# Retention and two MLPs on one core: the powers of lambda by running sums, the decay table through ScalarE's DMA queue, and a small factor table for r

## The chip, the cores and the metric

One core of a Trainium2 chip runs the whole program. The metric is device microseconds of that core; lower is better. A value is the median of several executions.

## The reference

Inputs q, k, v are [2 batches, 8 heads, 768 positions, 64], `lam` holds one decay per head (0.97 to 0.99), and two MLPs follow.

```python
Dmask = np.where(rel >= 0, lam[:, None, None] ** rel[None, :, :], 0.0)
...
intra = np.einsum('bhic,bhjc->bhij', qb, kb) * Dmask[None]
intra = np.einsum('bhij,bhjd->bhid', intra, vb)
inter = np.einsum('bhid,bhde->bhie', qb * lam_pow[None], kv_state)
out[:, :, sl] = intra + inter
kb_dec = kb * rev_pow[None]
kv_state = lam_block[None, :, None, None] * kv_state + np.einsum('bhsd,bhse->bhde', kb_dec, vb)
...
h = x @ w_in                                   # first MLP, 512 -> 2048
g = np.maximum(h, 0.0) + alpha * np.minimum(h, 0.0)
return (g @ w_out)                             # 2048 -> 512; the second MLP squares relu(h)
```

## The kernel before

Retention is done first, in 12 chunks n = 0 to 11 (six chunks of 128 positions for two batches, in turn). The two MLPs follow on the 1536 rows that retention left in SBUF as a high and a low part.

The names of one chunk: `k`, `q` (channels first) and `v`, `r` (positions first; `r` is k once more) are loads of 256 KB each on SyncE's queue. PE makes scores `s` (L422). DVE multiplies them by the decay table `dec` into `sc` (L434). PE multiplies `sc` by `v` into `o` (L459), adds the state's part from `q` times `grow` (L467), and makes the state's update `pk` from `r` and `v` (L477). ScalarE casts `o` to `xah` (L486), PE subtracts that from `o` (`less`, L495) and ScalarE casts the rest to `xal`. GpSimd multiplies `q` by `grow` (L441) and `r` by the last column of `dec` (L444).

The tables come from `lam`, which is loaded first. VectorE makes lambda^1, ^2, ^4 .. ^128 by seven squarings, corrects their rounding (L357 to L371), and multiplies them out into `z`, 8 rows (heads) of 256: 127 zeros and lambda^0 .. ^128. `z` goes to DRAM as `zd`, and `dec` is read back from there: partition p takes each head's 128 values from place p on, so 1024 pieces of 512 bytes. `grow` is made by PE from `z` (`pg`, L402) and copied out of PSUM by VectorE (L406).

The order on each engine is that of the code; nothing is rescheduled. SyncE and ScalarE issue the DMAs written for them in their own order, and an instruction that waits holds up all that stands behind it on its engine. A DMA raises one of eight semaphores, DMAHW0 to DMAHW7, given in turn; the next DMA on the same semaphore waits until the one before it on that semaphore has landed. The scores have two PSUM buffers, so `s` of chunk 2 waits until ScalarE has copied `s` of chunk 0 (L427). The load of `v` of chunk 1 waits for a one-column GpSimd copy of `grow` (L305), and so for `grow`; all loads of later chunks stand behind it on SyncE. `keep_warm(1)` puts 17 matmuls on zeros ahead of the first `o`.

Of the kernel before, what the change touches and what calls it, by code (L numbers as in the profile page):

```python
# [7 lines left out]
F32 = mybir.dt.float32  # L8
F32R = mybir.dt.float32r
# [3 lines left out]
ALU = mybir.AluOpType  # L13
PSUM = bass.MemoryType.PSUM

B, H, S, D = 2, 8, 768, 64
CH = 128
NCH = S // CH
NN = B * NCH
NPAIR = H // 2  # L20
# [6 lines left out]
ZW = 256  # L27
# [13 lines left out]
ORDER = [(n // B, n % B) for n in range(NN)]  # L41

LEAST = 2.0**-15
WARM = 12, 17
EARLY_UNITS = [0, 0, 0, 1, 0, 1, 0, 1, 0, 1, 1, 0]
EARLY_LOADS = [0, 1, 1, 0, 1, 0, 1, 0, 1, 1, 1, 1]

# [6 lines left out]
def retention_then_two_mlps(  # L54
# [15 lines left out]
    nc = tc.nc  # L70
# [199 lines left out]
    ap1 = actx.enter_context(tc.tile_pool(name="ap1", bufs=1))  # L270
# [6 lines left out]
    pso = actx.enter_context(tc.tile_pool(name="pso", bufs=2, space=PSUM))  # L277
# [3 lines left out]

    lam_sb = ap1.tile([H, 1], F32, name="lam_sb")
    nc.sync.dma_start(lam_sb, lam)
    NB = 8
    sq = ap1.tile([H, NB], F32, name="sq")
    z = ap1.tile([H, ZW], F32, name="z")
    nc.vector.memset(z[:, 0 : CH - 1], 0.0)
    ones, tens = ap1.tile([H, 8], F32, name="ones"), ap1.tile([H, 16], F32, name="tens")
    err = ap1.tile([H, NB], F32, name="err")
    nc.vector.memset(err[:, 0:1], 0.0)  # L290
    nc.vector.memset(ones[:, 0:1], 1.0)
    nc.vector.memset(tens[:, 0:1], 1.0)
    qk_t, vk_t = {}, {}

    def load_qk(n):
# [6 lines left out]
    def load_vk(n):  # L302
        v_t = kp.tile([128, H, D], F32, tag="v", name=f"v{n}")
        if n == 1:
            nc.gpsimd.tensor_copy(v_t[:, 0, 0:1], grow[:, 0, 0:1])  # L305
        nc.sync.dma_start(v_t, vr[n])
        r_t = None
        if ORDER[n][0] < NCH - 1:
            r_t = kp.tile([128, H, D], F32, tag="r", name=f"r{n}")
            nc.sync.dma_start(r_t, kr[n])  # L310
        vk_t[n] = v_t, r_t


    warm = ap1.tile([128, CH], F32, name="warm")
    nc.gpsimd.memset(warm, 0.0)

    def keep_warm(i):
        pw = pso.tile([128, NPAIR, CH], F32, tag="o", name=f"warm_ps{i}")
        for a in range(WARM[i]):
            nc.tensor.matmul(pw[:, a % NPAIR, :], warm, warm, start=True, stop=True)  # L320

    def where(name, shape, pattern, base, fill, channel=1):

        x = ap1.tile(shape, F32, name=name)
        zeros = warm[0 : shape[0], 0 : shape[-1]]
        if len(shape) == 3:
            zeros = zeros.unsqueeze(1).to_broadcast(shape)
        nc.gpsimd.affine_select(
            x, zeros, pattern=pattern, compare_op=ALU.not_equal, fill=fill, base=base,
            channel_multiplier=channel,  # L330
        )
        return x
# [6 lines left out]
    for t in range(2):  # L339
        m = where(f"head{t}", [H, NPAIR, D], [[-2, NPAIR], [0, D]], -t, 1.0)  # L340
        nc.gpsimd.tensor_copy(head[:, :, t], m)

    keep_warm(0)
    for n in range(FIRST):
        load_qk(n)

    nc.vector.tensor_copy(sq[:, 0:1], lam_sb)
    for b in range(1, NB):
        nc.vector.tensor_tensor(sq[:, b : b + 1], sq[:, b - 1 : b], sq[:, b - 1 : b], ALU.mult)
    top = ap1.tile([H, NB - 1], F32R, name="top")  # L350
    topf = top.bitcast(F32)
    low = ap1.tile([H, NB - 1], F32, name="low")
    twice = ap1.tile([H, NB], F32, name="twice")
    tmp = ap1.tile([H, NB - 1], F32, name="tmp")
    tmp2 = ap1.tile([H, NB - 1], F32, name="tmp2")
    a, p = sq[:, 0 : NB - 1], sq[:, 1:NB]
    nc.vector.tensor_copy(top, a)  # L357
    nc.vector.tensor_scalar(twice, sq, 2.0, None, ALU.mult)
    nc.vector.tensor_tensor(tmp, topf, topf, ALU.mult)
    nc.vector.tensor_tensor(low, a, topf, ALU.subtract)  # L360
    nc.vector.tensor_tensor(tmp, tmp, p, ALU.subtract)
    nc.vector.scalar_tensor_tensor(tmp2, low, 2.0, topf, ALU.mult, ALU.mult)
    nc.vector.tensor_tensor(tmp, tmp, tmp2, ALU.add)
    nc.vector.tensor_tensor(tmp2, low, low, ALU.mult)
    nc.vector.tensor_tensor(err[:, 1:NB], tmp, tmp2, ALU.add)
    for b in range(2, NB):
        nc.vector.scalar_tensor_tensor(
            err[:, b : b + 1], err[:, b - 1 : b], twice[:, b - 1 : b], err[:, b : b + 1],
            ALU.mult, ALU.add,
        )  # L370
    nc.vector.tensor_tensor(sq, sq, err, ALU.add)  # L371

    for b in range(4):
        for part, b0 in ((tens, 3), (ones, 0)):
            w = 1 << b
            if w < part.shape[1]:
                nc.vector.tensor_scalar(
                    part[:, w : 2 * w], part[:, 0:w], sq[:, b0 + b : b0 + b + 1], None, ALU.mult
                )
    nc.vector.tensor_tensor(  # L380
        z[:, CH - 1 : 2 * CH - 1].rearrange("h (i j) -> h i j", j=8),
        tens.unsqueeze(2).to_broadcast([H, 16, 8]),
        ones.unsqueeze(1).to_broadcast([H, 16, 8]),
        ALU.mult,
    )
    nc.vector.tensor_copy(z[:, ZW - 1 : ZW], sq[:, NB - 1 : NB])


    zd = dram.tile([H, ZW], F32, name="zd")
    dec = ap1.tile([128, H, CH], F32, name="dec")  # L390
    nc.sync.dma_start(zd, z)
    load_vk(0)
    nc.sync.dma_start(dec, bass.AP(zd[:, :].tensor, zd[:, :].offset, [[1, 128], [ZW, H], [1, CH]]))
    dec_v = dec.rearrange("p (a t) i -> p t a i", t=2)

    grow = ap1.tile([128, NPAIR, CH], F32, name="grow")

    def growth():
        pg = psk.tile([128, 2, NPAIR, D], F32, tag="pk", name="pg")
        pg = pg.rearrange("p a b c -> p (a b c)").rearrange("p (a i) -> p a i", i=CH)  # L400
        for a in range(NPAIR):
            nc.tensor.matmul(  # L402
                pg[:, a], head[:, a].rearrange("h t d -> h (t d)"), z[:, CH:ZW], start=True,
                stop=True,
            )
        nc.vector.tensor_copy(grow, pg)  # L406


    state = {}
# [26 lines left out]
    def factors(n):  # L436

        c = ORDER[n][0]
        if c > 0:
            q_t = qk_t[n][0]  # L440
            nc.gpsimd.tensor_tensor(q_t, q_t, grow, ALU.mult)  # L441
        if c < NCH - 1:
            r_t = vk_t[n][1]
            nc.gpsimd.tensor_tensor(  # L444
                r_t, r_t, dec[:, :, CH - 1 : CH].to_broadcast([128, H, D]), ALU.mult
            )

    old_t = {}
# [63 lines left out]
    for n in range(FIRST):  # L512
        scores(n)
        if n == 2:
            growth()
    keep_warm(1)
    load_vk(1)
    for n in range(2):
        factors(n)
    for n in range(DA):  # L520
        decay(n)
    for n in range(NN):
# [25 lines left out]
        if n + 2 < NN:  # L548
            factors(n + 2)
# [19 lines left out]
    for s in range(len(steps) + LAG):  # L569
        if s < len(steps):  # L570
            m, t, f, part = steps[s]
# [78 lines left out]
```

## Time and profile before

| | |
|---|---|
| median of 3 runs | 588.88 us (587.77 to 589.57) |
| span of the profiled execution | 585.6 us |
| PE busy | 578.3 us (99% of the span) |
| VectorE, ScalarE, GpSimd busy | 360.8, 296.3, 28.2 us |
| retention, up to the first matmul of the MLPs | 58.1 us |

The span runs from the first to the last instruction. The profiled execution's own time is not listed apart from its span; the median of the runs is 3.3 us above the span, which is what lies around it. Busy time is modelled for PE (its matmuls are pipelined), so the argument reads starts of matmuls rather than busy shares.

### The profile page before, as it was taken

The page shows a single profiled execution, that of the slowest core. Times are in us where ns is not written, and L with a number is a line of the kernel's source. Part 1 is how long each engine was busy: PE and PEld are TensorE (multiplying, and loading weights), DVE is VectorE, ACT ScalarE, POOL GpSimd, SP SyncE. Part 2 cuts the span into 40 slices and gives each one's busy share as a digit, 9 for nine tenths or more (in the row PEclk, how much of TensorE's full clock was granted, in tenths as well). Part 3 has the DMA queues.
Part 4 walks back from the last instruction along what each step waited for, and adds up shares of the span by engine and source line. Part 5 has one row for each costly group of instructions (what it writes and reads, how often), then busy time and mean ns, then how long its engine had stood idle before and what let it go on. Part 6 is the DMA issues. An engine that isn't in the chain of part 4 may idle for free.

```text
span 585.6 us, 7998 instructions
## 1 busy us (share of the span) xinstructions
PE 578.3 (99%) x3083; PEld 478.8 (82%) x3083; DVE 360.8 (62%) x616; ACT 296.3 (51%) x515; POOL 28.2 (5%) x31
## 2 busy tenths in 40 slices
PE   8999999999999999999999999999999999999997
PEld 8788788888888888888888888888888888888885
DVE  4787897677677777887887787676622222222422
ACT  2556768676646666576576564654522221322220
POOL 1862000000000000000000000000000000000000
PEclk9999999999999999999999999999999999999999
DMA  7992234322626232332432133332100000400401
GB/s 247 383 390 99 85 131 144 144 78 102 213 78 213 108 98 83 131 119 75 137 115 96 49 108 104 112 109 72 73 0 1 0 1 0 144 0 1 143 1 72
DMA packets 25733, 62.39 MB, mean 107 GB/s; under 512 B 2904, under 2 KB 3936, under 8 KB 25696
## 3 DMA queue, kind: packets, MB, share of 16 engines
q1 hardware_dynamic: 17632, 32.53, 15.7%
q10 hardware_dynamic: 8064, 29.36, 14.5%
q8 instruction: 24, 0.39, 0.3%
q14 instruction: 13, 0.11, 0.1%
HBM read 52.44 MB, written 9.45 MB: 106 GB/s over the span
## 4 chain that ended last, share of the span: by engine, by line
PE 92%; DVE 3%; DMA 2%; ACT 2%; issue 0%; ACTq 0%; DVEq 0%
PE h L172 43%; PE acc L225 22%; PE acc L227 22%; PE o L459 1%; PE o L467 1%; DMA dec<-zd 1%; DMA v<-in_vr_dram 1%; PE s L422 1%; PE pk L477 1%; DVE sc L434 1%; DVE bits L139 0%; PE o L495 0%; ACT bits L122 0%; ACT raw L123 0%; DVE bits L131 0%
## 5 line engine op out<-in xcount | busy, mean ns | idle before, releaser
L191 ACT CAST gh<-g 128x512 fp32r<-128x512 f32 x96 | 59.6, 621 | 92.6 <-DVE g L182 38.6
L182 DVE SCALAR_TENSOR_TENSOR g<-h,g 128x512 f32<-128x512 f32 x48 | 33.2, 691 | 117.2 <-ACT g L181 117.2
L181 ACT ACTIVATE g<-h 128x512 f32<-128x512 f32 x48 | 28.7, 597 | 124.9 <-PE h L172 124.9
L196 DVE TENSOR_TENSOR gl<-g,gh 128x512 fp32r<-128x512 f32 x96 | 66.5, 693 | 31.0 <-ACT gh L191 22.3
L225 PE MATMUL acc<-gh,wl 128*128 128x512 f32 x192 | 74.8, 390 | 0.7 <-ACT gh L191 0.7
L225 PE MATMUL acc<-gl,wh 128*128 128x512 f32 x192 | 74.8, 390 | 0.0
L172 PE MATMUL h<-xah,wl 128*128 128x512 f32 x192 | 74.8, 390 | 0.0
L225 PE MATMUL acc<-gh,wh 128*128 128x512 f32 x192 | 74.7, 389 | 0.0
L172 PE MATMUL h<-xah,wh 128*128 128x512 f32 x192 | 74.7, 389 | 0.0
L172 PE MATMUL h<-xal,wh 128*128 128x512 f32 x192 | 74.7, 389 | 0.0
L172 PE MATMUL h<-xbh,wl 128*128 128x512 f32 x192 | 74.7, 389 | 0.0
L172 PE MATMUL h<-xbl,wh 128*128 128x512 f32 x192 | 74.7, 389 | 0.0
L172 PE MATMUL h<-xbh,wh 128*128 128x512 f32 x192 | 74.7, 389 | 0.0
L227 PE MATMUL acc<-wl,gh 128*128 128x512 f32 x192 | 74.7, 389 | 0.0
L227 PE MATMUL acc<-wh,gh 128*128 128x512 f32 x192 | 74.7, 389 | 0.0
L227 PE MATMUL acc<-wh,gl 128*128 128x512 f32 x192 | 74.7, 389 | 0.0
L186 DVE SCALAR_TENSOR_TENSOR g<-h,g 128x512 f32<-128x512 f32 x42 | 29.0, 691 | 40.7 <-ACT g L185 40.5
L150 DVE TENSOR_TENSOR wl<-bits,wh 128x512 fp32r<-128x512 f32 x64 | 45.2, 706 | 3.9 <-ACT wh L141 3.8
L131 DVE SCALAR_TENSOR_TENSOR bits<-raw,bits 128x512 uint32<-128x512 uint32 x64 | 45.1, 705 | 2.2
L139 DVE CUSTOM_DVE_ANT_0 bits<-raw,bits 128x1024 uint16<-128x1024 uint16 x64 | 45.2, 707 | 0.0
L122 ACT ACTIVATE bits<-raw 128x512 f32<-128x512 f32 x64 | 43.1, 674 | 0.0
L225 PEld LDWEIGHTS acc<-gh,wl 128*128 128x128 f32 x192 | 36.0, 187 | 8.5 <-ACT gh L191 1.1
(81 smaller groups left out, 828.7 us busy)
## 6 DMA issues: line engine op xcount, KB each, us to landing
raw<-in_w_dram ACTq DMA_DIRECT2D x56, 512.0 KB, 3.3
ps<-sums SPq DMA_DIRECT2D x24, 256.0 KB, 3.3
sums<-p SPq DMA_DIRECT2D x20, 256.0 KB, 2.2
raw<-in_w_dram SPq DMA_DIRECT2D x8, 512.0 KB, 6.0
k<-in_kt_dram SPq DMA_DIRECT2D x12, 256.0 KB, 4.9
q<-in_qt_dram SPq DMA_DIRECT2D x12, 256.0 KB, 5.3
v<-in_vr_dram SPq DMA_DIRECT2D x12, 256.0 KB, 5.9
r<-in_kr_dram SPq DMA_DIRECT2D x10, 256.0 KB, 5.3
```

Source lines behind the costliest of these rows:

```text
L122: nc.scalar.activation(x.bitcast(F32), high.bitcast(F32), AF.Abs)
L131: nc.vector.scalar_tensor_tensor(x, high, 0xC0000000, x, ALU.bitwise_and, ALU.bitwise_or)
L139: nc.vector.tensor_tensor(x.bitcast(I32), x.bitcast(I32), low.bitcast(I32), ALU.add)
L150: nc.vector.tensor_tensor(lo, x, hi.bitcast(F32), ALU.subtract)
L172: nc.tensor.matmul(ph, w[:, cols], x[:, c, :], start=c == 0 and i == 0, stop=c == NC - 1 and i == 2)
L181: nc.scalar.activation(g, ph, AF.Relu)
L182: nc.vector.scalar_tensor_tensor(g, ph, 0.0, g, ALU.max, ALU.mult)
L186: nc.vector.scalar_tensor_tensor(g, ph, 0.0, g, ALU.max, ALU.subtract)
L191: nc.scalar.copy(gh, g)
L196: nc.vector.tensor_tensor(gl, g, gh.bitcast(F32), ALU.subtract)
L225: nc.tensor.matmul(acc[t][i], w[:, cols], g, **flags)
L227: nc.tensor.matmul(acc[t][i], g[:, cols], w, **flags)
```

## The change

Three things. The powers of lambda: a running sum along 128 columns (`tensor_tensor_scan`, each value is lambda times the one before plus a zero) makes them in one instruction; eight small instructions work out the rounding error of each step, a second running sum carries the errors on, and an addition writes `z`. The write of `zd` and the read of `dec` are issued by ScalarE, not by SyncE. And `r` is multiplied by a table `fade` [128, 8], which PE makes from `z` and an 8x8 identity (`pf`) behind `pg`, and VectorE copies out of PSUM behind `grow`. `keep_warm(1)` has 5 matmuls where it had 17.

```diff
-WARM = 12, 17
+WARM = 12, 5
...
-    nc.vector.tensor_copy(sq[:, 0:1], lam_sb)
-    for b in range(1, NB):
-        nc.vector.tensor_tensor(sq[:, b : b + 1], sq[:, b - 1 : b], sq[:, b - 1 : b], ALU.mult)
...
-    nc.vector.tensor_copy(z[:, ZW - 1 : ZW], sq[:, NB - 1 : NB])
+    lams = lam_sb.to_broadcast([H, CH])
+    before, after = power[:, 0:CH], power[:, 1 : CH + 1]
+    nc.vector.tensor_tensor_scan(after, lams, warm[0:H, :], 1.0, ALU.mult, ALU.add)
...
+    nc.vector.tensor_copy(lam_high, lam_sb)
+    nc.vector.tensor_copy(high, before)
+    lh, hf = lam_high.bitcast(F32), high.bitcast(F32)
+    nc.vector.tensor_tensor(lam_low, lam_sb, lh, ALU.subtract)
+    nc.vector.tensor_tensor(low, before, hf, ALU.subtract)
+    nc.vector.scalar_tensor_tensor(err, hf, lh, after, ALU.mult, ALU.subtract)
+    for x, y in ((low, lh), (hf, lam_low), (low, lam_low)):
+        nc.vector.scalar_tensor_tensor(err, x, y, err, ALU.mult, ALU.add)
+    nc.vector.tensor_tensor_scan(low, lams, err, 0.0, ALU.mult, ALU.add)
+    nc.vector.tensor_tensor(z[:, CH:ZW], after, low, ALU.add)
...
-    nc.sync.dma_start(zd, z)
+    nc.scalar.dma_start(zd, z)
     load_vk(0)
-    nc.sync.dma_start(dec, bass.AP(zd[:, :].tensor, zd[:, :].offset, [[1, 128], [ZW, H], [1, CH]]))
+    nc.scalar.dma_start(dec, bass.AP(zd[:, :].tensor, zd[:, :].offset, [[1, 128], [ZW, H], [1, CH]]))
...
+        pf = pso.tile([128, NPAIR, CH], F32, tag="o", name="pf")[:, 0, 0:H]
+        nc.tensor.matmul(pf, z[:, CH - 1 : ZW - 1], eye, start=True, stop=True)
+        nc.vector.tensor_copy(fade[:, :, 0], pf)
...
-                r_t, r_t, dec[:, :, CH - 1 : CH].to_broadcast([128, H, D]), ALU.mult
+                r_t, r_t, fade.to_broadcast([128, H, D]), ALU.mult
```

ScalarE from the program's start, before: the copies of the scores of chunks 0 and 1 stand right behind the cast of `less`.

```order
L336 CAST less_132<-lessf_128 128x128 [waits Pool_49]
L427 COPY sc0_234<-s0_225 128x1024 [waits PE_49]
L427 COPY sc1_245<-s1_236 128x1024 [waits PE_49]
L486 CAST xah0_84<-o0_310 128x4x128 [waits PE_49]
L504 COPY state0_1_222<-pk0_319 128x256 [waits PE_49]
```

The same place with the change:

```order
L332 CAST less_128<-lessf_124 128x128 [waits Pool_49]
L365 DMA zd_190<-z_117 8x256 [waits DMAHW3_49,DVE_49]
L367 DMA dec_191<-zd_190 128x8x128 [waits DMAHW4_49,DMAHW3_49]
L405 COPY sc0_213<-s0_204 128x1024 [waits PE_49]
L405 COPY sc1_224<-s1_215 128x1024 [waits PE_49]
L464 CAST xah0_84<-o0_280 128x4x128 [waits PE_49]
```

The two DMAs now stand ahead of both copies; the first waits for `z` (DVE) and for DMAHW3, the second for `zd` (DMAHW3) and for DMAHW4.

PE from the scores of chunk 1 to the first `o`, before:

```order
L422 MATMUL s1_236<-q1_162,k1_163 128x128 [waits DMAHW4_49,DMAHW3_49]
...
L422 MATMUL s2_247<-q2_166,k2_167 128x128 [waits DMAHW6_49,DMAHW5_49,Activation_49]
...
L402 MATMUL pg_257<-z_118,head_134 128x128 [waits DVE_49,Pool_49]
...
L422 MATMUL s3_263<-q3_170,k3_171 128x128 [waits DMAHW7_49,DMAHW0_49,Activation_49]
...
L320 MATMUL warm_ps1_273<-warm_126 128x128 x17
L459 MATMUL o0_310<-sc0_234,v0_215 64x128 [waits DMAHW2_49,DVE_49]
```

And with the change:

```order
L400 MATMUL s1_215<-q1_162,k1_163 128x128 [waits DMAHW4_49,DMAHW3_49]
...
L400 MATMUL s2_226<-q2_166,k2_167 128x128 [waits DMAHW6_49,DMAHW5_49,Activation_49]
...
L377 MATMUL pg_236<-z_117,head_130 128x128 [waits DVE_49,Pool_49]
...
L383 MATMUL pf_242<-eye_141,z_117 128x8 [waits Pool_49]
L400 MATMUL s3_245<-q3_170,k3_171 128x128 [waits DMAHW7_49,DMAHW0_49,Activation_49]
...
L316 MATMUL warm_ps1_255<-warm_122 128x128 x5
L437 MATMUL o0_280<-sc0_213,v0_193 64x128 [waits DMAHW1_49,DVE_49]
```

`pf` stands between `pg` and `s3`, and 12 of the matmuls on zeros are gone. DMAHW3 and DMAHW4 are those of the loads of `k1` and `q1`, in both kernels.

SyncE behind the load of `k3`, before:

```order
L299 DMA q3_170<-in_qt_dram 128x512 [waits DMAHW0_49]
L391 DMA zd_212<-z_118 8x256 [waits DMAHW1_49,DVE_49]
L306 DMA v0_215<-in_vr_dram 128x512 [waits DMAHW2_49]
L310 DMA r0_217<-in_kr_dram 128x512 [waits DMAHW3_49]
L393 DMA dec_213<-zd_212 128x8x128 [waits DMAHW4_49,DMAHW1_49]
L306 DMA v1_291<-in_vr_dram 128x512 [waits DMAHW5_49,Pool_49]
```

With the change:

```order
L295 DMA q3_170<-in_qt_dram 128x512 [waits DMAHW0_49]
L302 DMA v0_193<-in_vr_dram 128x512 [waits DMAHW1_49]
L306 DMA r0_195<-in_kr_dram 128x512 [waits DMAHW2_49]
L302 DMA v1_261<-in_vr_dram 128x512 [waits DMAHW5_49,Pool_49]
L306 DMA r1_264<-in_kr_dram 128x512 [waits DMAHW6_49]
```

SyncE no longer waits for `z`; `v0` and `r0` follow the load of `q3`, and `v1` still waits for GpSimd's copy of `grow`.

## Rows read from the trace of the kernel before

**Rows 1.** Stretches: each engine's busy us (x instructions), PE clock, DMA share, GB/s.

```profile
0.00:10.00 10.00, 8.32 (x77) 7.75 (x77) 5.28 (x37) 3.61 (x4) 2.22 (x10) 1.00 0.70 230
...
20.00:40.00 20.00, 20.00 (x315) 16.28 (x313) 15.07 (x19) 12.87 (x35) 14.07 (x13) 1.00 1.04 392
```

**Rows 2.** Timeline of PE from the first `o`: start, us, what [idle before].

```profile
15.62 0.66 PE L459 MATMUL o<-sc,v 128*64 128x128 f32 x8
16.95 0.66 PE L459 MATMUL o<-sc,v 128*64 128x128 f32 x8 [0.68 <-DVE sc L434]
...
19.00 1.09 PE L459 MATMUL o<-sc,v 128*64 128x128 f32 x16 [0.20 <-PE o L495]
19.90 0.66 PE L477 MATMUL pk<-v,r 128*64 128x64 f32 x16
...
33.04 1.16 PE L422 MATMUL s<-q,k 64*128 64x128 f32 x16
...
58.09 0.50 PE L172 MATMUL h<-xah,wl 128*128 128x512 f32 x1
```

**Rows 3.** The chain that ended last, in order of time: start, us, what.

```profile
0.74 1.31 DMA lam_sb<-in_lam_dram
...
7.85 1.87 DMA zd<-z
9.73 4.91 DMA dec<-zd
...
14.74 2.17 DVE sc L434 x2
```

**Rows 4.** Timeline of PE ahead of the first `o`.

```profile
0.99 4.42 PE L320 MATMUL warm_ps<-warm 128*128 128x128 f32 x24 [0.99 <-POOL warm L315]
...
8.36 1.16 PE L422 MATMUL s<-q,k 64*128 64x128 f32 x16 [0.20 <-DMA q<-in_qt_dram]
9.45 1.15 PE L402 MATMUL pg<-z,head 8*128 8x128 f32 x8
10.53 1.16 PE L422 MATMUL s<-q,k 64*128 64x128 f32 x16
11.62 4.06 PE L320 MATMUL warm_ps<-warm 128*128 128x128 f32 x34
```

**Rows 5.** Groups by form, 2 to 20 us: busy, mean ns | idle before.

```profile
L444 POOL TENSOR_TENSOR r<-r,dec 128x512 f32<-128x512 f32 x2 | 3.0, 1533 | 3.2 <-DMA dec<-zd 3.2
...
L427 ACT COPY sc<-s 128x1024 f32<-128x1024 f32 x2 | 2.0, 1012 | 4.9 <-PE s L422 4.9
...
L406 DVE COPY grow<-pg 128x512 f32<-128x512 f32 x1 | 0.7, 692 | 2.8 <-PE pg L402 2.8
...
L380 DVE TENSOR_TENSOR z<-tens,ones 8x128 f32<-8x128 f32 x1 | 0.3, 279 | 0.0
```

**Rows 6.** Timeline: loads of k1, v1, r1, q7; VectorE's copy of `grow`.

```profile
2.04 0.43 SPq L298 DMA_DIRECT2D k<-in_kt_dram  x1
...
10.64 0.69 DVE L406 COPY grow<-pg 128x512 f32<-128x512 f32 x1 [2.82 <-PE pg L402]
...
11.61 0.34 SPq L306 DMA_DIRECT2D v<-in_vr_dram  x1
...
11.99 0.42 SPq L310 DMA_DIRECT2D r<-in_kr_dram  x1
...
21.74 0.33 SPq L299 DMA_DIRECT2D q<-in_qt_dram  x1
```

**Rows 7.** DMA issues, 2.05 to 2.45 us (k1): KB each, us to landing.

```profile
k<-in_kt_dram SPq DMA_DIRECT2D x1, 256.0 KB, 3.8
```

**Rows 8.** DMA issues, 11.65 to 12.3 us (v1 and r1).

```profile
v<-in_vr_dram SPq DMA_DIRECT2D x1, 256.0 KB, 3.7
r<-in_kr_dram SPq DMA_DIRECT2D x1, 256.0 KB, 4.0
```

**Rows 9.** DMA issues, 21.8 to 22.05 us (q7).

```profile
q<-in_qt_dram SPq DMA_DIRECT2D x1, 256.0 KB, 7.3
```

More of the change, by code (lines that the diff above doesn't have):

```diff
@@ L283, in retention_then_two_mlps @@
     nc.sync.dma_start(lam_sb, lam)
-    NB = 8
-    sq = ap1.tile([H, NB], F32, name="sq")
     z = ap1.tile([H, ZW], F32, name="z")
     nc.vector.memset(z[:, 0 : CH - 1], 0.0)
[L288 to L292, printed above, removed]
+    nc.vector.memset(z[:, CH - 1 : CH], 1.0)
+    power = ap1.tile([H, CH + 1], F32, name="power")
+    nc.vector.memset(power[:, 0:1], 1.0)
     qk_t, vk_t = {}, {}
@@ L341, in retention_then_two_mlps @@
         nc.gpsimd.tensor_copy(head[:, :, t], m)
+    eye = where("eye", [H, H], [[-1, H]], 0, 1.0)
     keep_warm(0)
@@ L345, in retention_then_two_mlps @@
         load_qk(n)
-    nc.vector.tensor_copy(sq[:, 0:1], lam_sb)
-    for b in range(1, NB):
-        nc.vector.tensor_tensor(sq[:, b : b + 1], sq[:, b - 1 : b], sq[:, b - 1 : b], ALU.mult)
[L350 to L385, printed above, removed]
-    nc.vector.tensor_copy(z[:, ZW - 1 : ZW], sq[:, NB - 1 : NB])
+    lams = lam_sb.to_broadcast([H, CH])
+    before, after = power[:, 0:CH], power[:, 1 : CH + 1]
+    nc.vector.tensor_tensor_scan(after, lams, warm[0:H, :], 1.0, ALU.mult, ALU.add)
+    lam_high = ap1.tile([H, 1], F32R, name="lam_high")
@@ new lines, in retention_then_two_mlps @@
+    lam_low = ap1.tile([H, 1], F32, name="lam_low")
+    high = ap1.tile([H, CH], F32R, name="high")
+    low = ap1.tile([H, CH], F32, name="low")
+    err = ap1.tile([H, CH], F32, name="err")
+    nc.vector.tensor_copy(lam_high, lam_sb)
[4 more added lines that the diff above has]
+    nc.vector.scalar_tensor_tensor(err, hf, lh, after, ALU.mult, ALU.subtract)
@@ L394, in retention_then_two_mlps @@
     dec_v = dec.rearrange("p (a t) i -> p t a i", t=2)
     grow = ap1.tile([128, NPAIR, CH], F32, name="grow")
+    fade = ap1.tile([128, H, 1], F32, name="fade")
     def growth():
```

## Prediction

> **What bounds the kernel now.** I read the stretches first, then PE's timeline, the chain that ended last, and the landings of single loads. From 20 to 40 us PE is busy 20.00 of 20.00 us [rows 1]; the table of the page has it at 99% of the span. So PE sets the end of the MLPs, which begin at 58.09 [rows 2] and take 585.6 - 58.09 = 527.5 us, and it sets the pace of retention too once it has begun. The exception is the beginning. Second halves of the first `o` start at 16.95, after 0.68 us of waiting for VectorE's product with the decay table; from there on waits are short [rows 2]. The chain says what made that late [rows 3]: `lam` lands at 0.74 + 1.31 = 2.05, VectorE works until `zd` is issued at 7.85, `zd` takes 1.87 us, `dec` is issued at 9.73 and takes 4.91 us, and the products start at 14.74 and take 2.17 us: 16.91. The 17 matmuls on zeros, 11.62 to 15.62 [rows 2, 4], fill PE meanwhile and end before that chain does. Whatever the chain gains, everything behind 16.95 gains, unless another wait takes its place: PE's own row of work, ScalarE, or the loads.
>
> **What the change moves.** *VectorE.* Eleven instructions stand between `lam` and `z`. The one row of their size, 8x128, takes 0.279 us [rows 5]; with a little between them, 0.3 each, `z` is ready at 2.05 + 3.3 = 5.4. The running sums are not in the trace. Below I take them as that product, 0.28; above as the copy of four times as many columns, 0.692 [rows 5], which makes `z` 0.8 later, 6.2. [...]
>
> *The issue of zd.* It also waits for the semaphore that the load of `k1` raises (DMAHW3 in both listings). `k1` is issued at 2.04 and lands 3.8 us later [rows 6, 7]: 5.84. So not `z` but `k1` comes last, unless the sums are near their upper bound. `zd` is issued at 5.84 in place of 7.85, 2.01 earlier.
>
> *zd and dec.* At 1.87 us for `zd` as before, `dec` is issued at 5.84 + 1.87 + 0.02 = 7.73, against 9.73: 2.0 earlier. At 4.91 us for `dec` it lands at 12.64, and VectorE starts 0.10 later, as before: 12.74 against 14.74. Before, `dec` stood on SyncE's queue behind `v0` and `r0`; now these two stand in the other queue at the same time. I keep 4.91, since it was measured beside as many loads.
>
> *What ScalarE's wait holds up.* Both copies of scores stand behind the issue of `dec`. It ends some 0.4 after 7.73 (issues take 0.33 to 0.43 [rows 6]), the first copy takes 1.01 [rows 5], and `s2`, which needs its PSUM buffer, starts at about 9.2 in place of 8.36 [rows 4]. From `s2` to `grow` it was 10.64 - 8.36 = 2.28 us [rows 4, 6]: `grow` is copied from 11.5 to 12.2. `fade` follows; its copy costs between nothing and 0.28, the 8x128 row. VectorE is free at 12.45, just ahead of `dec`: hidden, by 0.2 us. If `dec` is quicker than 4.6 us, this chain is what remains, and the gain stops at 2.3.
>
> *PE.* `s2` 9.2, `pg` 10.3, `pf` 11.4 (at most a fourth of `pg`'s 1.08, 0.27), `s3` 11.65, matmuls on zeros at 12.75, in steps of 1.08 to 1.09 [rows 4]; five of them at 4.00 / 17 = 0.235 end at 13.9. The first half of `o` then ends at about 14.4, and the second half waits for VectorE until 12.74 + 2.17 + 0.04 = 14.95. Hidden by 0.5. With all 17, PE would have come to `o` at 16.75: without that part of the edit the gain would be 0.9 or so.
>
> *GpSimd and the loads.* `r0` needs only `fade`: 12.45 + 1.53 [rows 5] = 14.0, ahead of its matmuls near 15.4. `v1` is issued 0.28 after the end of `grow` as before [rows 6]: 12.45 in place of 11.61, and every load behind it as much later, 0.84. `r1`, issued 0.38 behind, landed after 4.0 with `dec` ahead of it [rows 6, 8]; now nothing of that queue is ahead. At 4.0 it lands at 16.8, its product ends at 18.4, and `pk1`, due at 19.90 - 2.0 = 17.9 [rows 2], is 0.5 late: the lower bound. I take about 3.3, which is in time. `v1` had 19.00 - (11.61 + 3.7) = 3.7 us to spare [rows 2, 6, 8], `q7` 33.04 - (21.74 + 7.3) = 4.0 [rows 2, 6, 9]; PE's 2.0 and the delay of 0.84 make 2.84. Loads stay hidden.
>
> **Sum.** zd's issue 2.0 earlier, zd and dec unchanged, VectorE, PE and GpSimd hidden: the second half of `o` moves from 16.95 to 14.95, and with it the MLPs. The span of 585.6 becomes 583.6. What lies around it I take as the same 3.3, so 588.9 at the median of the runs becomes 586.9. Bounds of this case: 1.5 (running sums slow, or `r1` late) to 2.3 (VectorE's chain, `dec` quicker), and half a microsecond more if `zd` alone in its queue needs only the 1.31 of `lam` [rows 3] and `dec` is quicker as well: 586.1 to 587.4.
>
> **Rivals.** *zd queues with the loads, slower.* At 5.84 some four loads are under way. If `zd` waits behind them on the same DMA engines, it takes what loads take there, 4.0 to 4.91 [rows 3, 8]; then `dec` is issued at 9.85 to 10.75, ScalarE holds both copies until then, and the end is 0.1 to 1.0 later: up to 589.9. It decides from 9.73 - 5.84 = 3.9 us on. For it: the engines are busy 0.70 of the first 10 us [rows 1]. Against it: `zd` took 1.87 even with loads ahead of it in its own queue. [...]
>
> *dec is bound by bytes.* Ten loads of 256 KB and `dec`'s 512 KB are 3.15 MB. At the first 10 us' 230 GB/s [rows 1] that ends at 13.7, and the gain shrinks to 14.64 - 13.7 = 0.9: 588.0. At 392 GB/s, as from 20 to 40, it ends 8 us after the start and binds nothing. The 230 holds the start and SyncE's wait for `z`, so I think it too low. [...]
>
> [...]
>
> *The loads set the pace.* DMA is at 1.04 from 20 to 40 [rows 1]. If the later issue of `v1` costs more than the 0.9 to 1.2 us left over of the margins, PE waits in chunks 1 to 5 and half the gain goes: 588.
>
> **Chances.** Forecast (gain 1.5 to 2.5) 0.62; more than that 0.04; zd queues 0.10; dec bound by bytes 0.10; clock 0.06; loads, `r1` or slow sums 0.08. A measurement of this kernel tells about 0.3%, 1.8 us, from no change, so the forecast itself lies just above that line: of its 0.62 I give 0.49 to faster, with the 0.04 above it 0.53. Slower by 1.8 us needs `zd` above 5.6 us or two rivals together: 0.08. The rest, 0.39, is the same. The range goes from the forecast's lower bound to the middle of the slower rival: 586.0 to 589.3.
>
> **What would show it.** Right: `zd` issued at 5.8 to 5.9 on ScalarE; `dec` issued near 7.7 and the first product with it near 12.7; second half of the first `o` near 15.0; first matmul of the MLPs near 56.1; no new waits in between. Wrong: `zd` above 3 us; VectorE at `grow` or `fade` when `dec` has long landed; a granted clock below 1.00; PE waiting for `r` or `v` in chunks 1 to 5.

## The result and the profile after

The changed kernel takes 592.84 us (median of 5 runs, 592.03 to 593.33) against 588.72 of the kernel before in the same runs (587.77 to 589.57): ratio 1.0067, interval [1.0056, 1.0078]. It is 4.1 us slower; 586.9 and a gain of 2.0 were forecast, and the range ended at 589.3. The profiled execution took 592.84 us with a span of 590.8.

The MLPs tell first where to look. Their first matmul, the answer to the last of [rows 2]:

```profile
62.83 0.50 PE L172 MATMUL h<-xah,wl 128*128 128x512 f32 x1
```

It stands at 62.83 in place of 58.09, 4.74 later; from there to the end of the span it is 528.0 us, 527.5 before, so 0.5 us of the span's 5.2 came in the MLPs. From the end of the first `o` (20.72 + 1.88 = 22.60 below, 16.95 + 0.66 = 17.61 in [rows 2]) to the MLPs it is 40.2 us, 40.5 before. So all the rest was lost ahead of the first `o`. No load sets PE's pace behind it: from 22 us to the MLPs PE waits 0.2 us in all. The timeline of PE there, to lay beside [rows 4]:

```profile
5.91 2.42 PE L400 MATMUL s<-q,k 64*128 64x128 f32 x32
12.07 2.06 PE L400 MATMUL s<-q,k 64*128 64x128 f32 x16 [3.74 <-ACT sc L405]
14.06 2.07 PE L377 MATMUL pg<-z,head 8*128 8x128 f32 x8
15.92 0.43 PE L383 MATMUL pf<-eye,z 8*128 8x8 f32 x2
16.28 2.08 PE L400 MATMUL s<-q,k 64*128 64x128 f32 x16
18.29 2.50 PE L316 MATMUL warm_ps<-warm 128*128 128x128 f32 x10
20.72 1.88 PE L437 MATMUL o<-sc,v 128*64 128x128 f32 x16
```

Two things are new: `s2` waits 3.74 us for a copy on ScalarE, and from there every group takes almost twice as long (2.07 in place of 1.15 for `pg`). The stretches say why (the last three figures are the granted clock, the DMA share and GB/s):

```profile
5.00:10.00 5.00, 3.23 (x39) 2.76 (x38) 0.46 (x2) 0.00 (x0) 0.00 (x0) 1.00 0.96 351
...
12.00:13.00 1.00, 0.93 (x8) 0.93 (x10) 0.00 (x0) 0.93 (x2) 0.00 (x0) 0.57 0.99 303
13.00:22.00 9.00, 9.00 (x60) 8.30 (x58) 5.84 (x7) 0.00 (x0) 3.00 (x3) 0.50 0.43 131
22.00:23.00 1.00, 1.00 (x24) 0.93 (x20) 0.37 (x1) 0.35 (x1) 1.00 (x2) 0.81 0.79 209
```

The granted clock is 1.00 until the pause ends, 0.57 between 12 and 13, 0.50 from 13 to 22, and rises after 22 (0.81 from 22 to 23). Now ScalarE, whose rows had nothing to show before, since `zd` and `dec` were SyncE's:

```profile
5.55 0.54 ACTq L365 DMA_DIRECT2D zd<-z  x1
10.55 0.41 ACTq L367 DMA_DIRECT2D dec<-zd  x1
11.01 1.93 ACT L405 COPY sc<-s 128x1024 f32<-128x1024 f32 x2 [8.68 <-DMA zd<-z]
```

`zd` is issued 2.30 earlier than in [rows 3], and `dec` 0.82 later: `zd` took 4.98 us, not 1.87. Both copies stood behind that wait, though the scores were done at 8.33. VectorE at that place (the last row is three products with `dec`):

```profile
5.21 0.28 DVE L361 TENSOR_TENSOR z<-power,low 8x128 f32<-8x128 f32 x1
16.16 0.69 DVE L381 COPY grow<-pg 128x512 f32<-128x512 f32 x1 [10.67 <-PE pg L377]
16.77 0.16 DVE L384 COPY fade<-pf 128x8 f32<-128x8 f32 x1
16.84 3.27 DVE L412 TENSOR_TENSOR sc<-sc,dec 128x512 f32<-128x512 f32 x3
```

The products no longer wait for `dec`, which took 3.8 us and lay there at 14.35; they stand behind `grow` and `fade`, 2.5 us later. And `o` no longer waits for them: PE comes to it at 20.72 without a gap since 12.07. So it is: `zd` late, ScalarE held, PE still, then the clock down, and PE's own row from `s2` to `o` takes 20.72 - 12.07 = 8.65 us, where 13.9 - 9.2 = 4.7 was forecast. The chain that ended last, the answer to [rows 3], goes the same way as far as `grow`:

```profile
5.55 4.98 DMA zd<-z
...
10.55 0.41 ACTq L367
...
11.01 1.02 ACT sc L405
...
12.07 2.06 PE s L400 x16
14.13 2.01 PE pg L377 x8
```

What `zd` waited for is seen in the DMA queues (q1 is SyncE's with the loads, q10 ScalarE's; packets, MB, share of 16 engines). A load of 256 KB is 128 packets of 2 KB. Of `zd`'s 16 packets (8 of 1 KB with its data, 8 of 4 bytes), issued at 5.55, none moves up to 8.00, 8 from 8 to 9, 6 from 9.0 to 9.5, 2 from 9.5 to 10. These are the answers for 5.5 to 7, 7 to 8, 8 to 9 and 9.0 to 9.5:

```profile
q1 hardware_dynamic: 300, 0.54, 100.5%
...
q1 hardware_dynamic: 180, 0.33, 93.7%
...
q1 hardware_dynamic: 210, 0.39, 101.2%
q10 hardware_dynamic: 8, 0.01, 1.6%
...
q1 hardware_dynamic: 111, 0.20, 105.3%
q10 hardware_dynamic: 6, 0.00, 1.6%
```

### The profile page after: what moved, and what is told of

The parts are those of the page before. It is cut to its first block, busy times and chain, and to the rows that moved or that the text cites. A ratio compares the mean times of both kernels' runs of the same rounds, so it can differ in the third digit from the quotient of the medians.

```text
span 590.8 us, 7930 instructions
## 1 busy us (share of the span) xinstructions
PE 580.8 (98%) x3061; PEld 481.3 (81%) x3061; DVE 357.9 (61%) x594; ACT 295.7 (50%) x515; POOL 27.7 (5%) x32
## 4 chain that ended last, share of the span: by engine, by line
PE 88%; DMA 6%; DVE 2%; ACT 1%; SPq 1%; issue 0%; POOL 0%; ACTq 0%
PE h L172 43%; PE acc L225 22%; PE acc L227 22%; DMA k<-in_kt_dram 2%; DMA v<-in_vr_dram 2%; DMA raw<-in_w_dram 1%; DMA r<-in_kr_dram 1%; DMA zd<-z 1%; DVE bits L131 0%; DVE bits L139 0%; DVE sc L412 0%; PE s L400 0%; PE pg L377 0%; ACT bits L122 0%; ACT raw L123 0%
```

## The experiments

Three theories stood at the start. **A**: `zd` waits for the loads that were issued before it, whichever queue it is in; its early issue buys little, and ScalarE's wait for it holds the copies and lets the clock fall. **B**: the other queue itself is what makes `zd` slow (a fixed price of ScalarE's queue). **C**: the 12 matmuls on zeros that are gone bring the clock down. Beside them stood the question how much of the 4.1 us is the clock. Each kernel was timed beside the kernel before, whose median was 588.55 to 588.72 us; a ratio below 1 is faster.

| run | median us | ratio and interval |
|---|---|---|
| e1, both tables on SyncE | 587.76 | 0.9982 [0.9972, 0.9992] |
| e2, `dec` issued behind the copies | 587.53 | 0.9983 [0.9974, 0.9993] |
| e3, zeros in PE's pause | 589.49 | 1.0013 [1.0002, 1.0023] |
| e4, change with squarings | 593.22 | 1.0077 [1.0055, 1.0100] |
| e5, five zeros alone | 589.06 | 1.0010 [0.9999, 1.0022] |
| e6, `zd` behind four loads | 589.53 | 1.0016 [1.0007, 1.0025] |
| e7, `zd` behind six loads | 587.35 | 0.9977 [0.9959, 0.9996] |
| e8, `fade` alone | 588.49 | 0.9989 [0.9978, 0.9999] |
| e9, e2 with four zeros | 587.79 | 0.9988 [0.9975, 1.0002] |
| e10, e7 with r0 ahead of v0 | 587.45 | 0.9974 [0.9962, 0.9987] |
| e11, running sums alone | 588.15 | 0.9990 [0.9979, 1.0000] |
| e12, other queue alone | 594.75 | 1.0093 [1.0070, 1.0117] |

**e1, tables back on SyncE.** The rest of the change stays.

```diff
-    nc.scalar.dma_start(zd, z)
+    nc.sync.dma_start(zd, z)
     load_vk(0)
-    nc.scalar.dma_start(dec, ...)
+    nc.sync.dma_start(dec, ...)
```

> The changed kernel with zd and dec back on SyncE's queue, zd ahead of v0 and dec behind r0; all else as changed. Theory A (zd waits on the DMA engines behind every load issued before it, whichever queue it is in; in the changed kernel ScalarE stands still meanwhile and the hole on PE brings the clock down): zd is issued at 5.5, lands only near 9, dec near 13.5 to 14, ScalarE copies from 6.9 on, the clock stays at 1.00, time 587.8 to 588.9, close to the kernel before. Rival B (ScalarE's queue is slow in itself, the loads have no part): zd takes under 2.5 us on SyncE, dec is issued before 8.2 and the time is 587 or less. Rival C (the 12 matmuls on zeros that are gone bring the clock down): clock below 1.00 here too and 590 or more.

587.76. The chain that ended last has

```profile
5.51 4.54 DMA zd<-z
...
10.07 4.82 DMA dec<-zd
```

In SyncE's own queue `zd` takes 4.54: B falls. With nothing of ScalarE's held, 5.1 us of the time are gone. The clock didn't stay at 1.00, as A had it: PE waits 2.19 us for the products with `dec` ahead of the first `o`, and behind that the clock is low for some 3 us:

```profile
16.85:18.00 1.15, 1.15 (x21) 1.03 (x16) 1.15 (x2) 0.70 (x2) 1.15 (x1) 0.50 1.01 369
```

So C has a part here, though not the time of 590 that it named. Each execution lists its mean granted clock: the six of e1's ten with 0.997 take 587.71 to 588.74 us, the four with 0.999 or 1.000 take 586.56 to 587.24.

**e2, only the issue of `dec` moved**, behind the two copies on ScalarE; `zd` stays in ScalarE's queue.

```diff
-    nc.scalar.dma_start(dec, ...)
...
     for n in range(FIRST):
         scores(n)
+        if n == 1:
+            nc.scalar.dma_start(dec, ...)
```

> The changed kernel with the issue of dec put behind ScalarE's copies of the scores of chunks 0 and 1; zd stays on ScalarE ahead of them. Theory A: zd still takes about 5 us and dec is issued near 10.5 and lands near 14.3, but s2 starts at about 8.4, grow is copied near 10.7, the clock stays at 1.00; first products near 14.5, time 588.2 to 589.0. If the late zd alone made the loss and the hold of ScalarE had no part, the time stays near 592.8.

587.53, better than either theory had it. In the profiled execution (586.06 us, the fastest of ten) `zd` takes 4.37 and `dec` 4.42; `o` starts at 15.26 and the MLPs at 56.54. So the hold, with all that it brings about, costs 592.84 - 587.53 = 5.3 us. The clock falls here as well, which A didn't expect:

```profile
10.00:15.00 5.00, 4.53 (x32) 3.99 (x30) 1.25 (x3) 0.00 (x0) 1.19 (x2) 0.66 0.82 239
```

**e9, e2 with zeros between the scores**, so that the clock stays.

```diff
-WARM = 12, 5
+WARM = 12, 5, 4
...
         if n == 1:
+            keep_warm(2)
             nc.scalar.dma_start(dec, ...)
```

> The kernel in which the issue of dec stands behind ScalarE's two copies of scores, with four matmuls on zeros more, between the scores of chunk 1 and of chunk 2. If the clock that fell there from 10.98 to 14.40 us cost nothing, because the first products waited for dec until 14.52 anyway, the time stays at that kernel's 587.5 (587.2 to 587.8) while the granted clock stays at 1.00. If the clock did cost something there, the time falls to 586.0 to 587.0.

The time is the same within the intervals, 587.79, and the clock is 1.00 throughout in the profiled execution (the mean is 1.000 in six of ten executions, where e2 has it in one of ten). So that fall of the clock costs nothing that the medians show: PE waits for `dec` there anyway.

**e3, zeros in PE's pause** of the changed kernel, which leaves the hold as it is.

```diff
-WARM = 12, 5
+WARM = 12, 5, 16
...
         scores(n)
+        if n == 1:
+            keep_warm(2)
```

> The changed kernel with 16 more matmuls on zeros between the scores of chunk 1 and of chunk 2, so that PE works while ScalarE waits; zd and dec as changed. Theory A: the clock stays at 1.00 from its first rise on, s2 still starts near 12.1, from s2 to the copy of grow 2.3 us in place of 4.1, second half of the first o near 17.4, time 589.0 to 589.7, so some 3.5 of the 4.1 lost are the clock's. If the clock has no part (the hold alone makes the loss): 592.5 or more.

589.49. PE's timeline and the stretches:

```profile
8.47 3.84 PE L316 MATMUL warm_ps<-warm 128*128 128x128 f32 x32
12.24 1.16 PE L400 MATMUL s<-q,k 64*128 64x128 f32 x16
13.34 1.15 PE L377 MATMUL pg<-z,head 8*128 8x128 f32 x8
...
10.00:15.00 5.00, 5.00 (x55) 4.74 (x55) 0.47 (x1) 1.93 (x2) 0.00 (x0) 1.00 0.37 111
15.00:20.00 5.00, 4.78 (x73) 4.16 (x69) 5.00 (x7) 1.88 (x7) 2.61 (x3) 1.00 0.50 184
```

`s2` starts as late as in the changed kernel, but at a granted clock of 1.00, and `o` follows at 16.95, 4.71 us behind it: 592.84 - 589.49 = 3.35 of the 4.1 us are the clock. The other 0.8 is what e3 loses to the kernel before. It isn't the whole price of the hold: against e2, which has neither the hold nor these zeros, e3 loses 589.49 - 587.53 = 1.96, and up to 0.5 of that may be the zeros, which end at 12.3 where ScalarE's first copy ends at 11.7.

**The four parts alone**, each in the kernel before. e11: the running sums, nothing else. e12: `zd` and `dec` by ScalarE, nothing else. e8: `r` multiplied by `fade`, nothing else. e5: five zeros in place of 17.

```diff
 e11: the squarings replaced by the running sums, as in the change
 e12:
-    nc.sync.dma_start(zd, z)
+    nc.scalar.dma_start(zd, z)
-    nc.sync.dma_start(dec, ...)
+    nc.scalar.dma_start(dec, ...)
 e8: eye, pf and fade, as in the change
 e5:
-WARM = 12, 17
+WARM = 12, 5
```

> The kernel before with the running sums alone: zd and dec on SyncE as before, 17 matmuls on zeros, r multiplied by the column of dec. If zd waits for the ten loads that were issued before it, it is issued at 5.5, takes 4.2 to 4.8 us, dec is issued near 10.0 and the products start at 14.7 to 15.1: 588.5 to 589.3, no change, though z is 2.3 us earlier. If the powers themselves were on the path, as the prediction has it, zd takes 1.9 to 2.5, dec is issued at 7.5 to 8.1, and the time is 586.6 to 587.4.

> The kernel before with the other queue alone: zd and dec issued by ScalarE, squarings, 17 matmuls on zeros, r multiplied by the column of dec. If ScalarE's wait for zd holds both copies of scores, dec is issued near 10.6, the copies start near 11.1, PE stands still for 2.5 to 4 us, the clock falls, and the longer row of zeros comes after it: 593 to 595.5. If the hold costs only what dec's later issue does, 0.9 us: 589.3 to 590.0.

> The kernel before with r multiplied by fade, nothing else (squarings, SyncE's queue, 17 matmuls on zeros). Theory D (in the kernel before, the first products on VectorE and the products of r on GpSimd start together when dec lands, and slow one another; with fade those of r are done before): the three first products take 2.4 to 2.8 us in place of 4.16, second half of the first o 0.5 to 0.8 earlier, time 587.7 to 588.3. Rival: GpSimd's products do not matter, time 588.5 to 589.

> The kernel before with 5 matmuls on zeros in place of 17, nothing else. Theory A (PE's wait of some 3 us ahead of the first o is enough to bring the clock down, as it came down at 16.85 in the kernel with the tables on SyncE): clock at its lower level for a stretch near 15 to 19, time 589.3 to 590.5. Rival: the 12 matmuls are of no use, clock at 1.00, time 588.3 to 588.9.

e11 gives 588.15, between the two forecasts; its profile has `zd` as A says. The two issues on SyncE:

```profile
5.51 0.30 SPq L364 DMA_DIRECT2D zd<-z  x1
9.70 0.38 SPq L366 DMA_DIRECT2D dec<-zd  x1
```

`z` is ready 2.3 us earlier, and `dec` is issued 0.03 earlier than in [rows 3]. The interval of the ratio reaches 1, so a gain of the running sums by themselves isn't shown; in this one execution the MLPs begin at 59.24.

e12 alone costs 6.2 us. ScalarE and PE:

```profile
7.84 0.54 ACTq L391 DMA_DIRECT2D zd<-z  x1
11.08 0.41 ACTq L393 DMA_DIRECT2D dec<-zd  x1
11.54 1.93 ACT L427 COPY sc<-s 128x1024 f32<-128x1024 f32 x2 [9.21 <-DMA zd<-z]
12.60 1.37 PE L422 MATMUL s<-q,k 64*128 64x128 f32 x16 [4.01 <-ACT sc L427]
```

e8 speeds up VectorE's first products, 2.43 against 4.16 for three, since GpSimd is no longer beside them; but in the profiled execution `dec` took 6.74 us, and the median gains 0.2 us where 0.4 to 1.0 was expected. e5 costs 0.3 us at the median, less than expected, and its interval reaches 1. Its clock fell all the same (0.58 from 15 to 20), behind a wait of 3.22 us for the products with `dec`. The one execution of ten with a mean clock of 1.00 took 587.84, the others 588.11 to 590.09: the zeros that are gone do have a price, which the median shows in part. The four ratios add up to -0.1 + 0.9 - 0.1 + 0.1 = 0.8% against the change's 0.67%. The queue is the only part that loses clear of noise, and by itself it loses more than the whole change.

**e4, the change with the squarings of before**, so that `z` comes at 7.8 again.

```diff
-    nc.vector.tensor_tensor_scan(after, lams, warm[0:H, :], 1.0, ALU.mult, ALU.add)
+    nc.vector.tensor_copy(sq[:, 0:1], lam_sb)
...
```

> The changed kernel with the powers made by squarings as before, so that z is ready at 7.8 in place of 5.5; queue, fade and five matmuls on zeros as changed. Theory A: zd, issued 2.3 later behind the same eight loads and v0 and r0, lands when these have, near 10.5 to 11, so the earlier z bought nothing and the time is that of the changed kernel, 592.5 to 593.5. Rival B (a first DMA on ScalarE's queue takes a fixed 5 us): zd lands near 12.8 and the time is 2 us above the changed kernel, about 595.

593.22 (4 runs), 0.4 above the changed kernel and within the intervals of both. `zd` is issued 2.30 later, takes 2.81, and `dec` is issued at 10.68 against 10.55. So even in the changed kernel the running sums bring almost nothing.

**e6 and e7, `zd` ahead of some loads.** SyncE's order becomes k0 q0 k1 q1 `zd` k2 q2 `dec` k3 q3 v0 r0 in e6, and k0 q0 k1 q1 k2 q2 `zd` k3 q3 `dec` v0 r0 in e7. The edit is that of e7; in e6 the first loop ends at 2, `load_qk(2)` stands behind `zd`, and `load_qk(3)` behind `dec`.

```diff
-    for n in range(FIRST):
+    for n in range(3):
         load_qk(n)
...
-    nc.scalar.dma_start(zd, z)
-    load_vk(0)
-    nc.scalar.dma_start(dec, ...)
+    nc.sync.dma_start(zd, z)
+    load_qk(3)
+    nc.sync.dma_start(dec, ...)
+    load_vk(0)
```

> Running sums, fade and 5 zeros as changed; zd and dec on SyncE, with zd ahead of the loads of chunks 2 and 3 (four loads issued before it), then k2, q2, dec, k3, q3, v0, r0. Theory A (zd waits for the loads issued before it): zd takes 1.5 to 2.2 us, dec is issued at 7.2 to 7.8, the first products start at 11.5 to 12.3, time 585.5 to 587. Rival B (zd takes over 4 us whatever stands before it): dec issued near 10, time 588 or more.

> As the kernel with four loads ahead of zd, but with the loads of chunk 2 ahead of it too (six): then k3, q3, dec, v0, r0. Theory A: zd lands when q2 has, 8.2 to 8.6, so it takes 2.7 to 3.1 us, dec is issued near 8.4 and the first products start at 11.6 to 12.5; no hole on PE, since s2 is not late; time 585.2 to 586.5. Rival B as there.

`zd` is even quicker than expected: 1.29 with four loads ahead, 2.01 with six. But `dec`, issued at 6.89 and 7.60, takes over 5 us: the products start at 12.91 in both, 0.4 to 0.6 behind the forecasts. And the times, 589.53 and 587.35, are above theirs. What now comes last is a load. In the chain of e6 it is q3:

```profile
5.52 1.29 DMA zd<-z
...
7.94 6.23 DMA q<-in_qt_dram
...
14.31 2.08 PE s L402 x16
```

In e6 SyncE waits with `zd` for `z` before it issues the loads behind it, so k2 goes out at 5.86 where the changed kernel has it at 3.01, and the DMA engines are 0.18 busy from 5.5 to 7. PE waits 1.49 us for q2 and then 2.68 us for q3; the clock falls near 11.7, as the second wait begins, and is low until some 18.5 (0.67 from 10 to 15, 0.65 from 15 to 20):

```profile
12.00:18.00 6.00, 3.69 (x24) 3.50 (x25) 5.04 (x7) 0.00 (x0) 2.38 (x4) 0.50 1.03 362
```

All ten executions of e6 have a mean clock of 0.993 or 0.994. What e6 would take without that fall was not run.

In the chain of e7 it is r0 that comes last:

```profile
5.51 2.01 DMA zd<-z
...
8.64 5.59 DMA r<-in_kr_dram
...
14.38 1.87 POOL r L423
```

The median of e7 hides two groups: the six executions with a mean clock of 0.998 or more take 585.99 to 587.45 us (the profiled one is the slowest of them), half of them inside the forecast of 585.2 to 586.5. The four with 0.993 or 0.997 take 587.92 to 590.05. What brings the clock down in those four has no trace.

**e10, e7 with r0 loaded ahead of v0.**

```diff
+        if n == 0:
...
+            nc.sync.dma_start(r_t, kr[n])
         nc.sync.dma_start(v_t, vr[n])
...
```

> The kernel in which zd stands behind six loads on SyncE, and r0 is loaded ahead of v0. There pk0 waited 1.38 us for the product of r0, whose load was issued at 8.64. If r0's place in the queue set that, r0 is issued near 8.0 and lands 0.6 earlier, the wait shrinks to 0.3 to 0.8, v0 comes 0.4 later than it did, and the time falls from 587.35 to 586.4 to 587.0. If the engines' bytes set the landing of both, the wait only changes its place: 587.1 to 587.7.

587.45: the wait changes its place. Now it is v0 that comes last:

```profile
5.51 2.96 DMA zd<-z
...
9.60 6.24 DMA v<-in_vr_dram
...
15.98 1.08 PE o L441 x7
```

`zd` took 2.96 here and 2.01 in e7, behind the same six loads; why is open.

e1, e2, e7, e9 and e10 differ in what waits for what, and all end at 587.35 to 587.79. That bytes bound them all (ten loads and `dec`) isn't shown, and the traces speak against it: from 10 to 12 us the DMA engines are 0.53, 0.44 and 0.19 busy in e1, e2 and e9, from 8 to 10 us 0.67 and 0.61 in e7 and e10. All five have lower medians than both kernels; the interval of e9 reaches 1, and those of the other four overlap, so no order among them is shown.

## Why the prediction was wrong

**Right.** The bottleneck and the place: all that was lost lies ahead of the first `o`. `z` at 5.4 (5.49). `zd`'s issue also waits for `k1`: 5.84 forecast, 5.55 measured, since `k1` landed after 3.41; in e9, where it took 4.08, `zd` was issued at 6.22 with `z` long ready. The running sums, 0.61 and 0.41, lay inside their bounds (0.28 and 0.692). `r0` (ready at 17.54 + 1.49 = 19.03, `pk0` starts at 22.44) and the loads behind `grow`: hidden. PE from `s2` to `o` at a clock of 1.00: 4.7, and 4.71 in e3.

**The step that failed** is "At 1.87 us for `zd` as before, `dec` is issued at 5.84 + 1.87 + 0.02 = 7.73". The 1.87 was measured for a `zd` that came at 7.85, when most of the loads ahead of it had gone. It isn't the price of `zd` but, for the most part, what was left of those loads. The runs show this: issued at about 5.5, it takes 1.29 behind four loads, 2.01 and 2.96 behind six (e7, e10), 4.2 and 4.5 behind eight in SyncE's queue (e11, e1); issued at 5.55 to 6.22 it takes 4.3 to 5.0 in ScalarE's queue with ten in the other (e2, e3, e9, the change). With eight or ten loads ahead, the moment at which it is done, 9.7 to 11.1, hardly moves with the moment at which `z` is ready. The packets say the same: when the first packet of `zd` started, the 2 KB packets of 4.0 loads had started in e6, of 5.6 and 6.2 in e7 and e10, of 7.4 to 8.1 with eight ahead in its own queue (before, e1, e5, e8, e11), and of 8.3 to 9.5 of the ten in the other queue (the change, e2, e3, e4, e9, e12).

The prediction weighed this as a rival and gave it 0.10; against it stood that `zd` had taken 1.87 with loads ahead of it in its own queue, the same 1.87 that misled the sum. The trace shows the wait itself: none of `zd`'s packets moved from 5.55 to 8.00, while the other queue had 480 (300 and 180 in the rows above), 30 for each of the 16 engines on average. The second queue shortened nothing either: 4.2 and 4.5 us behind eight loads in SyncE's queue, 4.3 to 5.0 in ScalarE's with ten in the other.

**The rivals' price was off too.** "zd queues with the loads" was priced at 0.1 to 1.0 us, the delay of `dec` alone (issued at 9.85 to 10.75, which held: 10.55), and the clock had a chance of its own, 0.06. No run shows a ground for that 0.06; what the runs show is a small price with five zeros alone (e5: a granted clock of 0.58 from 15 to 20 us, 0.3 us at the median), and in the changed kernel a fall that the first rival brought about: ScalarE held to 10.96 let PE stand for 3.74 us, and with zeros in that pause the clock stayed at 1.00 (e3). e3 splits what came: 0.8 against the kernel before with the hold alone, inside its price, and 3.35 for the clock, which was at 0.50 to 0.57 from 12 to 22 us while PE did `s2`, `pg`, `s3`, the zeros and the first `o`. In the kernel before, the clock was 1.00 behind waits of 0.2 to 0.7 us [rows 2, 4], not of 3.74.

**dec bound by bytes**, the rival with 588.0, didn't decide here, and no run shows it as the bound. In e6 and e7, once `zd` was quick, the products came at 12.91, nearly as forecast for the change (12.74), and a load was late in their place. At the median 0.8 to 1.4 us of the forecast's 2.0 was to be had, in the five kernels. In the six executions of e7 whose clock held it was all there: their median of 586.5 is 2.2 below the kernel before.

**A size** in the sum: 3.3 us around the span. Every profiled execution whose own time is listed has 1.9 to 2.1 (592.84 - 590.8 here), so the profiled execution of before lay about 1.3 below its median. That moved nothing in the argument. And a remark of the sum has the wrong sign: with all 17 zeros PE would come to `o` at 16.75 and to its second half at about 17.25, which is 0.3 behind the 16.95 of before and not a gain of 0.9. No run has the change with 17 zeros, and nothing rests on it.

## What to carry to other kernels

The duration of a small transfer in a trace can be mostly what was left of the loads issued before it (`zd`, 8 KB: 1.29 us in e6, 4.98 in the change): before an issue is moved earlier, count the bytes ahead of it, and take the duration as a moment of landing, not as a length. Before a DMA that waits for something is put on a compute engine's queue, list what that engine does next and let that wait be as long as the transfer can get (here ScalarE's copies began at 11.01, with the scores done at 8.33); with the issue behind the engine's urgent work, e2 took 587.53 where the change took 592.84. The same holds for the queue of the loads: a transfer that waits there for its data keeps back every load behind it (in e6 k2 went out at 5.86, in the change at 3.01). A pause that one step causes and the clock's fall that follows it are one case with one chance, and its price is the lower clock for all that PE does until the clock is back (3.35 us here), unless PE waits for something else anyway (587.53 with the fall in e2, 587.79 in e9). Where executions of one kernel differ, look at the granted clock of each before the median is explained by one trace (e7).

## What was not expected of the hardware

GpSimd's and VectorE's products took longer beside each other. With no GpSimd beside most of them, VectorE's first three products take 2.43 us, and GpSimd's first product of `r`, with no VectorE product beside it, 1.04 (e8). In the kernel before, where both start on `dec`, three take 4.16 and two of `r` 3.03; in the changed kernel, with one product of `r` beside, 3.27 and 1.49. The rows of VectorE and GpSimd in e8:

```profile
16.75 2.43 DVE L439 TENSOR_TENSOR sc<-sc,dec 128x512 f32<-128x512 f32 x3 [5.08 <-DMA dec<-zd]
...
12.01 1.04 POOL L449 TENSOR_TENSOR r<-r,fade 128x512 f32<-128x512 f32 x1 [0.16 <-DMA r<-in_kr_dram]
```

Not every product of VectorE was slower: one whose scores come from PSUM (`s` in place of `sc`) took as long beside GpSimd as without it, 1.23 and 1.22. Why the two kinds differ was not shown. In the kernel before, the first of these two has GpSimd at work beside it and the second has not:

```profile
21.70 1.23 DVE L434 TENSOR_TENSOR sc<-s,dec 128x1024 f32<-128x1024 f32 x1 [0.53 <-PE s L422]
...
49.98 1.22 DVE L434 TENSOR_TENSOR sc<-s,dec 128x1024 f32<-128x1024 f32 x1
```

`dec`, the same 512 KB each time, took between 3.8 us (changed kernel, e4, e12) and 6.74 (e8). In the three with 3.8 no load moves beside it, in e8 1.08 MB do; but in e3 it took 4.9 with none beside it, so loads aren't the whole of it, and the rest was not tried.
